# A token mixer on one core: zero products in one run, two blocks' factors made singly, a mask and the last factors later

## The chip, the cores and the metric

One Trainium2 chip, one of its cores. The metric is the device time of one execution in microseconds (us). Five engines work side by side, each through its own queue in order: TensorE (matrix products), VectorE, ScalarE, GpSimd and SyncE (which issues transfers). In the profile they are PE (with PEld for its weight loads), DVE, ACT, POOL and SP.

## The reference, cut to what matters

```python
x = A_x                                   # [1, 2048, 512], bf16
g = sigmoid((x * gate_w).sum(-1))         # a gate for each token
X = rfft2(x) * (w_r + 1j * w_i)
a = irfft2(X)                             # spectral filter over tokens and channels
h = layernorm(x, axis=-1)                 # each token over its 512 channels, eps 1e-5
u = gelu(einsum("bsd,sf->bdf", h, w1) + b1)      # token MLP, 2048 -> 1792
b = (einsum("bdf,fs->bds", u, w2) + b2)          # 1792 -> 2048, transposed back
out = g * a + (1 - g) * b
```

The change touches the layer norm's factors, the order in which normalised blocks are made for the first product of the MLP, and the tables of sines for the transforms.

## The kernel before

The 2048 tokens are 16 blocks of 128 (one token for each of the 128 partitions), 512 channels wide. The schedule is written by hand: an engine runs its instructions in the order in which the program issues them.

**Normalised blocks.** `hn[b]` is block b of the layer norm. VectorE takes the statistics of a block (`bstat`, L246) and joins them to mean and variance (`bn_aggr`, L253). The reciprocal root is a power on GpSimd (L258). Blocks 0 to 5 are normalised on VectorE (`norm_dve`, L271). For blocks 6 to 15 `aggr` and `norm` work on two blocks at a time, and ScalarE makes `hn` (L267) with a scale `rstd` and a bias `nmr` for each token. For the pairs (6, 7) and (14, 15) the constant is added and `nmr` is made on VectorE (L255, L264); for the others both are done on GpSimd, in four small steps: constant (L255), negative mean (L257), power (L258), product (L262).

**First product.** `mm1(b, ft)` multiplies block b of `w1` with `hn[b]` and adds it into column tile `ft` of `u1`. Blocks 0 to 11 go in the order of blocks, eight column tiles each; then each column tile, 0, 2, 4, 6, 1, 3, 5, 7, takes blocks 12 to 15 and goes through GELU on ScalarE (L354). So the first column tile needs blocks 12, 13, 14 and 15 within four products.

**Ahead of it** stand eight products of zeros (`pw`, L240), with one small product among them (`pb`, L239) that turns the first layer's biases into a column. ScalarE copies it to `bcol` (L301).

**Sines.** The transforms need tables `TD` and `TA`. Their angles are whole numbers, cut to a range by a mask on VectorE (`mask`, L195: `md` for TD, `ma` and `mc` for TA), and ScalarE takes the sine (`sines_d`, `sines_a`: L198, L201). These stand between the normalised blocks on ScalarE's queue.

**The gate.** `gprod(q)` (L279) multiplies x with the gate's weights on VectorE, four blocks for each call; ScalarE adds it up later.

Behind the first product TensorE goes through the rest of the first layer (L458), the transforms' products and the second layer (L468, L800) in an order that `fill` and `fill_to` fix by a modelled clock when the program is built.

Of the kernel before, what the change touches and what calls it, by code (L numbers as in the profile page):

```python
# [15 lines left out]
P = 128  # L16
S = 2048
D = 512
NB = 16
# [3 lines left out]
NDVE = 6  # L23
# [20 lines left out]
def kernel(  # L44
# [13 lines left out]
    nc = tc.nc  # L58
# [15 lines left out]
    def pair(name):  # L74
        return psum.tile([P, 2, 512], F32, tag="pair", name=name, bufs=3)

    def bank(name):
        return psum.tile([P, 512], F32, tag="mm", name=name, bufs=2)
# [23 lines left out]
    def gather_w(i):  # L102
        w = (A_w_r, A_w_i)[i]
        for o, src, idx in ((wn[:, i, 8:16].rearrange("p e l -> p (e l)"), w.rearrange("(c e) l -> c (e l)", e=8), 0),
                            (wn[:, i, 16], w, 1)):
            nc.gpsimd.indirect_dma_start(out=o, out_offset=None, in_=src,
                                         in_offset=bass.IndirectOffsetOnAxis(ap=widx[:, idx:idx + 1], axis=0))
# [36 lines left out]
    warm = small.tile([P, P], BF16, name="warm")  # L144
# [14 lines left out]
    def iota(dst, pattern, base, cm=0):  # L159
        nc.gpsimd.iota(dst, pattern=pattern, base=base, channel_multiplier=cm,  # L160
                       allow_small_or_imprecise_dtypes=True)
# [19 lines left out]
    def gather_rows():  # L181
        gp = nc.gpsimd
        iota(widx[:, 0:1], [[0, 1]], 255, -2)
        gp.tensor_scalar(wf[:, 0:1], acol[:, 0:1], 63.5, 1016.0, op0=Alu.is_ge, op1=Alu.mult)
        gp.tensor_scalar(wf[:, 1:2], acol[:, 0:1], 0.5, -1024.0, op0=Alu.is_lt, op1=Alu.mult)
        gp.tensor_scalar(wf[:, 2:3], acol[:, 0:1], -16.0, 2048.0, op0=Alu.mult, op1=Alu.add)
        gp.tensor_add(wf[:, 0:1], wf[:, 0:1], wf[:, 1:2])
        gp.tensor_add(wf[:, 0:1], wf[:, 0:1], wf[:, 2:3])
        gp.tensor_copy(widx[:, 1:2], wf[:, 0:1])
# [4 lines left out]
    def mask(m, n):  # L194
        nc.vector.tensor_single_scalar(m, m, n - 1, op=Alu.bitwise_and)  # L195

    def nsin(dst, m, n):
        nc.scalar.activation(dst, m, ActF.Sin, bias=c_mpi, scale=2.0 * PI_IN / n)  # L198

    def psin(dst, m, n):  # L200
        nc.scalar.activation(dst, m, ActF.Sin, bias=c_pi, scale=-2.0 * PI_IN / n)  # L201
# [5 lines left out]
    def sines_d():  # L207
        nsin(TD[:, :, 1], md[:, 1], 1024)
        nsin(TD[:, :, 2], md[:, 0], 1024)
        psin(TD[:, :, 0], md[:, 0], 1024)  # L210

    def angles_a(v):
        mask(ma[v][:], 2048)
        if v == 0:
            mask(mc[:], 2048)

    def sines_a(v):
        if v == 1:
            nsin(TA[:, :, 1], ma[1][:], 2048)
        else:  # L220
            nsin(TA[:, :, 2], ma[0][:], 2048)
            psin(TA[:, :, 0], ma[0][:], 2048)
            nsin(TA[:, 0, 2, 0:1], mc[:], 2048)
            psin(TA[:, 0, 0, 0:1], mc[:], 2048)
# [9 lines left out]

    pw = bank("pw")
    pb = bank("pb")
    for n in range(8):
        if n == 7:
            nc.tensor.matmul(pb[:, 0:NFT], lhsT=brow[:], rhs=ident[0:NFT, 0:NFT], start=True, stop=True)  # L239
        nc.tensor.matmul(pw[:].rearrange("p (n k) -> p n k", n=4), lhsT=warm[:],  # L240
                         rhs=warm[:, None, :].to_broadcast([P, 4, P]), start=True, stop=True)
    pu = [pair(f"u1_{i}") for i in range(3)]
    u1 = [pu[ft // 2][:, ft % 2] for ft in range(6)] + [bank("u1_6")[:], bank("u1_7")[:]]

    def bstat(b):
        nc.vector.bn_stats(out=stats[:, b, :], in_=xh[b // 8][:, b % 8, :])  # L246

    def on_dve(b):
        return b <= NDVE or b == NB - 2

    def aggr(b0, b1):
        for b in range(b0, b1):
            nc.vector.bn_aggr(out=mv[:, b, :], in_=stats[:, b, :])  # L253
        eng = nc.vector if on_dve(b0) else nc.gpsimd
        eng.tensor_scalar(mv[:, b0:b1, 1], mv[:, b0:b1, 1], 1e-5, 0.0, op0=Alu.add, op1=Alu.add)  # L255
        if not on_dve(b0):
            nc.gpsimd.tensor_scalar(nmr[:, b0:b1], mv[:, b0:b1, 0], -1.0, 0.0, op0=Alu.mult, op1=Alu.add)  # L257
        nc.gpsimd.tensor_tensor(rstd[:, b0:b1], mv[:, b0:b1, 1], c_mhalf.to_broadcast([P, b1 - b0]), op=Alu.pow)  # L258

    def norm(b0, b1):  # L260
        if not on_dve(b0):
            nc.gpsimd.tensor_mul(nmr[:, b0:b1], nmr[:, b0:b1], rstd[:, b0:b1])  # L262
        else:
            nc.vector.scalar_tensor_tensor(nmr[:, b0:b1], mv[:, b0:b1, 0], -1.0, rstd[:, b0:b1],  # L264
                                           op0=Alu.mult, op1=Alu.mult)
        for b in range(b0, b1):
            nc.scalar.activation(hn[:, b, :], xh[b // 8][:, b % 8, :], ActF.Identity,  # L267
                                 bias=nmr[:, b:b + 1], scale=rstd[:, b:b + 1])

    def norm_dve(b):  # L270
        nc.vector.tensor_scalar(hn[:, b, :], xh[0][:, b, :], mv[:, b, 0:1], rstd[:, b:b + 1],  # L271
                                op0=Alu.subtract, op1=Alu.mult)
# [5 lines left out]
    def gprod(q):  # L278
        nc.vector.tensor_mul(prod[q // 2][:, 4 * (q % 2):4 * (q % 2) + 4],  # L279
                             xh[q // 2][:, 4 * (q % 2):4 * (q % 2) + 4],  # L280
                             gwb[:, None, :].to_broadcast([P, 4, D]))
# [30 lines left out]
    for b in range(2, NDVE):  # L312
        bstat(b + 1)
        norm_dve(b)
        if b + 1 < NDVE:
            aggr(b + 1, b + 2)
    for b in range(NDVE, NB, 2):
        if b > NDVE:
            bstat(b)
        if b == NDVE + 2:  # L320
            norm(b - 2, b)
            sines_d()
        bstat(b + 1)
        aggr(b, b + 2)
        if b == NDVE:
            mask(md[:], 1024)
        if b == NB - 2:
            angles_a(1)
        if b > NDVE:
            norm(b, b + 2)  # L330
        if b == NB - 6:
            angles_a(0)
            sines_a(0)
# [3 lines left out]
            mm1(b, ft)  # L337
    for q in range(4):
        gprod(q)
    gather_rows()  # L340
    gather_w(0)
    gather_w(1)
# [30 lines left out]
    for g in range(2):  # L373
        for n, (ps, ms) in enumerate(zip(PLUS[g], MINUS[g])):
            w = 4 // len(PLUS[g])
# [419 lines left out]
    b = NB - 1  # L795
    for h0, h1 in ((0, 256), (256, 384), (384, 512)):
        hs = slice(h0, h1)
        y = bank("yb")
        for ft in range(NFT):
            nc.tensor.matmul(y[:, 0:h1 - h0], lhsT=w2t[b // 2][:, ft, P:2 * P], rhs=gl[:, ft, hs],  # L800
                             start=(ft == 0), stop=(ft == NFT - 1))
# [30 lines left out]
```

## Time and profile before

| | us |
|---|---|
| three timed runs | 128.85, 129.69, 129.98 |
| their median | 129.69 |
| the profiled execution | 128.63 |
| its span (first to last instruction) | 126.7 |
| TensorE busy in it | 122.3 |
| VectorE busy | 111.6 |
| ScalarE busy | 89.7 |
| GpSimd busy | 39.6 |

Times in the profile count from the start of the span. A matrix product's duration holds a modelled end (0.38 us for one of 512 columns, while the next starts 0.216 us behind it), so starts say more than durations. A line of the timeline gives start, duration (from the first start to the last end where several are merged, "x7"), engine, line of the program, operation, out<-in, shapes; in brackets stands the idle time of the engine ahead of it and who ended it.

### The profile page before, as it was taken

To read this page: it belongs to the slowest core of one execution; us is meant where nothing else is said; L and a number is where in the kernel's file an instruction comes from. 1 tells how busy PE (TensorE), PEld (TensorE's weight loads), DVE (VectorE), ACT (ScalarE), POOL (GpSimd) and SP (SyncE) were. 2 spreads that over 40 slices of the span, in tenths; PEclk is the share of its full clock that TensorE was granted. 3 is DMA by queue.
4 is the path that set the end of the run, shared out by engine and by line. 5 is a ranking of instruction groups with operands and counts; after the bars stand their busy time and mean duration, and the time that the engine had idled before them with its cause. 6 is when DMAs were issued, how large, how long until landed. Compare 5 with 4: busy or idle time off the path is not lost.

```text
span 126.7 us, 2074 instructions
## 1 busy us (share of the span) xinstructions
PE 122.3 (97%) x750; PEld 65.2 (51%) x750; DVE 111.6 (88%) x190; ACT 89.7 (71%) x137; POOL 39.6 (31%) x67
## 2 busy tenths in 40 slices
PE   6999999999999999999999999999999999999990
PEld 2244444444444576557764765477644444444480
DVE  4799998999999999999999999999999999993140
ACT  4391299999897699998994799229785599522420
POOL 7133288998887198000040000000000000261200
PEclk9999999999999999999999999999999999999998
DMA  3899999998899999999579206710021101269991
GB/s 95 268 327 379 368 374 352 292 309 262 206 276 121 320 290 293 290 287 291 143 220 294 65 0 190 228 42 0 0 79 50 41 3 41 83 82 201 175 224 29
DMA packets 34635, 24.05 MB, mean 190 GB/s; under 512 B 5536, under 2 KB 32032, under 8 KB 34624
## 3 DMA queue, kind: packets, MB, share of 16 engines
q1 hardware_dynamic: 32516, 21.02, 60.4%
q0 software_dynamic: 1936, 2.76, 13.0%
q8 instruction: 6, 0.10, 0.3%
q10 hardware_dynamic: 172, 0.13, 0.3%
q14 instruction: 5, 0.04, 0.1%
HBM read 19.15 MB, written 3.67 MB: 180 GB/s over the span
## 4 chain that ended last, share of the span: by engine, by line
PE 97%; DVE 0%; issue 0%
PE yb L468 36%; PE u L275 22%; PE u L458 16%; PE ivt L657 5%; PE ivd L673 3%; PE pw L240 3%; PE dp L525 3%; PE yb L800 2%; PE tok L516 2%; PE tok L517 2%; PE ivt L651 0%; PE tok L513 0%; DVE tbv L802 0%; DVE warm L145 0%; PE pb L239 0%
## 5 line engine op out<-in xcount | busy, mean ns | idle before, releaser
L468 PE MATMUL yb<-gl,w2t 128*128 128x512 bf16 x210 | 47.4, 379 | 0.0
L468 PEld LDWEIGHTS <-w2t 128*128 128x128 bf16 x210 | 20.2, 98 | 22.1
L275 PE MATMUL u<-hn,w1a 128*128 128x512 bf16 x128 | 28.5, 385 | 0.0
L458 PE MATMUL u<-hn,w1b 128*128 128x512 bf16 x96 | 23.3, 379 | 0.0
L448 ACT ACTIVATE tbv<-yb,ombb,omg 128x512 bf16<-128x512 f32 x15 | 11.6, 775 | 15.3 <-PE yb L468 15.1
L275 PEld LDWEIGHTS <-w1a 128*128 128x128 bf16 x128 | 12.7, 99 | 15.9 <-issue 1.5
L778 POOL DMA_DIRECT2D out_dram<-ap x3 | 4.0, 1528 | 49.2 <-DVE ap L773 45.3
L458 PEld LDWEIGHTS <-w1b 128*128 128x128 bf16 x96 | 9.0, 98 | 8.0
L286 ACT ACTIVATE junk<-prod 128x512 bf16<-128x512 bf16 x16 | 10.1, 631 | 0.3
L354 ACT ACTIVATE gl<-u,bcol 128x512 bf16<-128x512 f32 x14 | 9.2, 688 | 1.3 <-PE u L458 0.8
L629 ACT CAST R<-ivt 128x1024 bf16<-128x1024 f32 x8 | 7.8, 1038 | 2.3 <-PE ivt L657 2.3
L258 POOL TENSOR_TENSOR rstd<-mv,consts 128x2 f32<-128x2 f32 (+1 forms) x9 | 6.3, 703 | 8.1 <-DVE mv L255 8.0
L629 ACT CAST H<-ivd 128x1024 bf16<-128x1024 f32 x7 | 6.9, 1047 | 0.8 <-PE ivd L673 0.8
L787 DVE TENSOR_TENSOR tbv<-tbv,ap 128x512 bf16<-128x512 bf16 x3 | 1.3, 425 | 5.5 <-ACT tbv L448 5.5
L246 DVE BATCH_NORM_STATS2 stats<-xa 128x6 f32<-128x512 bf16 x8 | 5.5, 686 | 0.5 <-DMA xa<-in_A_x_dram 0.5
L267 ACT ACTIVATE hn<-xb,nmr,rstd 128x512 bf16<-128x512 bf16 x8 | 5.8, 802 | 0.0
L547 DVE TENSOR_TENSOR tatb<-PMA,wn 128x1024 bf16<-128x1024 bf16 x8 | 5.0, 690 | 0.2 <-issue 0.2
L246 DVE BATCH_NORM_STATS2 stats<-xb 128x6 f32<-128x512 bf16 x8 | 5.2, 676 | 0.0
L267 ACT ACTIVATE hn<-xa,nmr,rstd 128x512 bf16<-128x512 bf16 x2 | 1.5, 804 | 5.1 <-DVE nmr L264 5.1
L673 PEld LDWEIGHTS <-R 128*128 128x128 bf16 x64 | 3.8, 98 | 2.5 <-ACT R L629 2.5
L547 DVE TENSOR_TENSOR tatb<-PMB,wn 128x2048 bf16<-128x2048 bf16 x4 | 4.7, 1226 | 0.2
L518 ACT CAST ZA<-tok 128x1024 bf16<-128x1024 f32 x4 | 4.0, 1019 | 1.4 <-PE tok L517 1.3
(198 smaller groups left out, 225.8 us busy)
## 6 DMA issues: line engine op xcount, KB each, us to landing
w2t<-in_B_w_dram SPq DMA_DIRECT2D x8, 896.0 KB, 9.8
w1b<-in_B_w_dram SPq DMA_DIRECT2D x3, 1024.0 KB, 16.3
w1a<-in_B_w_dram SPq DMA_DIRECT2D x2, 1024.0 KB
out_dram<-tbv SPq DMA_DIRECT2D x14, 128.0 KB, 4.0
out_dram<-ap POOLq DMA_DIRECT2D x3, 512.0 KB, 6.8
w1a<-in_B_w_dram SPq DMA_DIRECT2D x4, 256.0 KB, 4.4
w1a<-in_B_w_dram SPq DMA_DIRECT2D x2, 512.0 KB, 8.0
xb<-in_A_x_dram SPq DMA_DIRECT2D x2, 512.0 KB, 7.3
```

What stands on the lines that cost most here:

```text
L246: nc.vector.bn_stats(out=stats[:, b, :], in_=xh[b // 8][:, b % 8, :])
L267: nc.scalar.activation(hn[:, b, :], xh[b // 8][:, b % 8, :], ActF.Identity, bias=nmr[:, b:b + 1], scale=rstd[:, b:b + 1])
L275: nc.tensor.matmul(u1[ft], lhsT=w1a[b // 4][:, b % 4, ft * P:(ft + 1) * P], rhs=hn[:, b, :], start=(b == 0), stop=(b == NB - 1))
L286: nc.scalar.activation(junk[:], prod[b // 8][:, b % 8], ActF.Copy, accum_out=glog[:, b:b + 1])
L354: nc.scalar.activation(gl[:, ft, :], src, ActF.Gelu_apprx_tanh, bias=b1f[:, ft:ft + 1], scale=1.0)
L448: nc.scalar.activation(tbv[0][:, b], y[:], ActF.Identity, bias=gate["ombb2"][:, b:b + 1], scale=gate["omg"][:, b:b + 1])
L458: nc.tensor.matmul(u[:], lhsT=w1b[c][:, b, k * P:(k + 1) * P], rhs=hn[:, b, :], start=(b == 0), stop=(b == NB - 1))
L468: nc.tensor.matmul(y[:], lhsT=w2t[b // 2][:, ft, (b % 2) * P:(b % 2 + 1) * P], rhs=gl[:, ft, :], start=(ft == 0), stop=(ft == NFT - 1))
L547: mul(tt[:, i, :, r:r + n], PM[:, 2 * s:2 * s + 2, r:r + n], w[:, None].to_broadcast([P, 2, n, 256]))
L629: nc.scalar.copy(out, pr[:].rearrange("p h n -> p (h n)"))
L657: nc.tensor.matmul(o[:, 2 * v:2 * v + 2], lhsT=UV[:, 2 * v + c, r, par::2], rhs=TB[:, s, c:c + 2], start=(c == 0), stop=(c == 1))
L673: nc.tensor.matmul(pr[:, c, o * P:(o + 1) * P], lhsT=plane(par, cos), rhs=TI[:, lst, t], start=True, stop=True)
```

## The change

Four edits:

1. The zero products: eight of full width (512 columns) in a row, then the biases' product, then a ninth zero product of half width. Before, the biases' product stood between the seventh and the eighth.
2. Block 6 and block 7 get their factors singly. Block 6 is joined, and its constant added on VectorE, straight behind `norm_dve(5)`; its `nmr` stays on VectorE. Block 7 is joined behind `norm(6)`, and its constant, `nmr` and product go to GpSimd.
3. The mask of `md` moves from behind the aggregates of blocks 6 and 7 to behind those of 8 and 9, and the sines of TD on ScalarE from ahead of `hn[8]` to behind `hn[9]`.
4. `norm(14, 16)`, which makes `nmr` for the last two blocks on VectorE and `hn` on ScalarE, moves out of the loop to behind the first gate product. On ScalarE's queue that is behind the last sines (`sines_a(1)`), which stood behind it before.

```diff
     pw = bank("pw")
     pb = bank("pb")
-    for n in range(8):
-        if n == 7:
+    for n in range(9):
+        w = 4 if n < 8 else 2
+        if n == 8:
             nc.tensor.matmul(pb[:, 0:NFT], lhsT=brow[:], rhs=ident[0:NFT, 0:NFT], start=True, stop=True)
-        nc.tensor.matmul(pw[:].rearrange("p (n k) -> p n k", n=4), lhsT=warm[:],
-                         rhs=warm[:, None, :].to_broadcast([P, 4, P]), start=True, stop=True)
+        nc.tensor.matmul(pw[:, 0:w * P].rearrange("p (n k) -> p n k", n=w), lhsT=warm[:],
+                         rhs=warm[:, None, :].to_broadcast([P, w, P]), start=True, stop=True)
...
     for b in range(2, NDVE):
         bstat(b + 1)
         norm_dve(b)
-        if b + 1 < NDVE:
-            aggr(b + 1, b + 2)
-    for b in range(NDVE, NB, 2):
-        if b > NDVE:
-            bstat(b)
-        if b == NDVE + 2:
-            norm(b - 2, b)
-            sines_d()
+        aggr(b + 1, b + 2)
+    bstat(NDVE + 1)
+    norm(NDVE, NDVE + 1)
+    aggr(NDVE + 1, NDVE + 2)
+    norm(NDVE + 1, NDVE + 2)
+    for b in range(NDVE + 2, NB, 2):
+        bstat(b)
         bstat(b + 1)
         aggr(b, b + 2)
-        if b == NDVE:
+        if b == NDVE + 2:
             mask(md[:], 1024)
         if b == NB - 2:
             angles_a(1)
-        if b > NDVE:
+        if b < NB - 2:
             norm(b, b + 2)
+        if b == NDVE + 2:
+            sines_d()
         if b == NB - 6:
             angles_a(0)
             sines_a(0)
     sines_a(1)
...
     for q in range(4):
         gprod(q)
+        if q == 0:
+            norm(NB - 2, NB)
```

(`NDVE` is 6, `NB` is 16.)

## The prediction

> **What bounds the kernel now.** I read the page first, then the chain of waits, then the timeline of TensorE, ScalarE, VectorE and GpSimd over the first 40 us. The page and its chain:
>
> ```profile
> span 126.7 us, 2074 instructions
> PE 122.3 (97%) x750; PEld 65.2 (51%) x750; DVE 111.6 (88%) x190; ACT 89.7 (71%) x137; POOL 39.6 (31%) x67
> ...
> PE 97%; DVE 0%; issue 0%
> ```
>
> The chain that ended last is TensorE alone. So an edit on another engine counts only where it makes TensorE wait or takes a wait away, and a wait of TensorE, once there, stays to the end. The timeline of TensorE over the first 40 us (start, duration, both in us), and then single pieces of it from narrow windows:
>
> ```profile
> 0.98 3.17 PE L240 MATMUL pw<-warm 128*128 128x512 bf16 x7 [0.98 <-DVE warm L145]
> 4.08 0.19 PE L239 MATMUL pb<-ident,brow 14*128 14x14 bf16 x1
> 4.20 0.61 PE L240 MATMUL pw<-warm 128*128 128x512 bf16 x1
> 4.82 28.50 PE L275 MATMUL u<-hn,w1a 128*128 128x512 bf16 x128
> ```
>
> ```profile
> 4.82 1.01 PE L275 MATMUL u<-hn,w1a 128*128 128x512 bf16 x2
> 6.05 0.63 PE L275 MATMUL u<-hn,w1a 128*128 128x512 bf16 x2
> 15.37 0.59 PE L275 MATMUL u<-hn,w1a 128*128 128x512 bf16 x2
> 15.89 0.38 PE L275 MATMUL u<-hn,w1a 128*128 128x512 bf16 x1
> 26.68 0.38 PE L275 MATMUL u<-hn,w1a 128*128 128x512 bf16 x1
> 26.89 0.38 PE L275 MATMUL u<-hn,w1a 128*128 128x512 bf16 x1
> ```
>
> A duration holds a modelled end, so I go by starts. Seven zero products begin (3.17 - 0.63)/6 = 0.42 us apart; the pair at 4.82 is 1.01 - 0.63 = 0.38 apart; the pair at 6.05 is 0.63 - 0.38 = 0.25 apart; from there all are 0.216 apart. So TensorE runs at half rate until about 6.1 us. The first real product starts at 4.82 because block 0 of hn ends at 4.35 + 0.41 = 4.76 (VectorE, L271). After that there is one hole in the first layer: the second product of the pair at 15.37 starts at 15.58, the next is due at 15.80 and comes at 15.89. It is the first of block 6, and hn of block 6 is what it waits for. The last two lines are the first column's products of blocks 14 and 15: due at 26.68 and 26.89, and not late.
>
> ScalarE, which makes hn from block 6 on:
>
> ```profile
> 15.03 1.52 ACT L267 ACTIVATE hn<-xa,nmr,rstd 128x512 bf16<-128x512 bf16 x2 [5.06 <-DVE nmr L264]
> 16.45 1.10 ACT L198 ACTIVATE TD<-md,consts 128x384 bf16<-128x384 int32 x2
> 17.46 0.60 ACT L201 ACTIVATE TD<-md,consts 128x384 bf16<-128x384 int32 x1
> 17.97 2.92 ACT L267 ACTIVATE hn<-xb,nmr,rstd 128x512 bf16<-128x512 bf16 x4
> 20.79 1.13 ACT L198 ACTIVATE TA<-ma,consts 128x1024 bf16<-128x1024 int32 x1
> 21.83 1.14 ACT L201 ACTIVATE TA<-ma,consts 128x1024 bf16<-128x1024 int32 x1
> ...
> 23.24 2.92 ACT L267 ACTIVATE hn<-xb,nmr,rstd 128x512 bf16<-128x512 bf16 x4
> 26.06 1.14 ACT L198 ACTIVATE TA<-ma,consts 128x1024 bf16<-128x1024 int32 x1
> ```
>
> Block 6 is ready at 15.03 + 0.80 = 15.83, hence the hole at 15.80. From 15.03 ScalarE has no free moment until after 27.2: sines of TD at 16.45, blocks 8 to 11, sines of TA, blocks 12 to 15 (the last ends at 23.24 + 2.92 = 26.16, 0.7 ahead of its use at 26.89), and the last sines at 26.06. One hn starts 0.705 after the one before, one TD sine 0.506, one TA sine 1.04.
>
> **The change, part by part.**
>
> *Zero products.* Eight in a row end at 3.51 + 2 x 0.427 = 4.37. The biases' product came 0.14 after its predecessor could have ended (4.08 against 3.94) and the next product 0.12 behind it: 4.51, 4.63. A half width product at half rate takes 0.213: 4.84. The first real product is then at 4.84 instead of 4.82: +0.02. The copy of the biases on ScalarE (4.31, 0.17 long) moves to about 4.74; the next on its queue is the root for block 1 at 5.62, so nothing waits. What the filled hole (4.63 to 4.82) does to the clock the trace can't say. Bounds: if full rate came at the first real product instead of at 6.1, 1.3 us at half rate would be saved half, 0.65, but block 2 of hn is ready only at 8.27 + 0.41 = 8.68, and block 6 is then reached at 8.74 + 4 x 1.727 = 15.65: -0.24 at most against 15.89. Late: at the end of the span the clock record halves between 125.5 and 125.6, 2.2 behind the last product (123.3); if full rate came that much later, +1.1. I take 0, since the start of the first real product hardly moves.
>
> [...]
>
> *Block 6 alone.* Its mean and variance are joined at 12.67, the constant is added at 12.88 (offsets as at 11.32 and 11.53), GpSimd's power (0.55 for one column) ends at 13.66, VectorE's nmr at 13.86, hn runs 13.90 to 14.70 instead of to 15.83. The hole of 0.09 goes: -0.09 for TensorE up to here.
>
> *Block 7 alone, through GpSimd.* Its aggregate starts 0.08 behind nmr at 13.78 and ends 13.95. GpSimd's four steps are added once more: in the trace, for two columns, they take 1.43:
>
> ```profile
> 17.91 0.23 POOL L255 TENSOR_SCALAR mv<-mv 128x2 f32<-128x2 f32 x1
> 18.21 0.19 POOL L257 TENSOR_SCALAR nmr<-mv 128x2 f32<-128x2 f32 x1
> 18.36 0.70 POOL L258 TENSOR_TENSOR rstd<-mv,consts 128x2 f32<-128x2 f32 x1
> 19.14 0.20 POOL L262 TENSOR_TENSOR nmr<-nmr,rstd 128x2 f32<-128x2 f32 x1
> ```
>
> With 0.55 for the power and 0.09 to get there, nmr of block 7 is ready at 15.36 and hn runs 15.40 to 16.20. TensorE wants it at 17.5: no cost.
>
> *Blocks 8 and 9 ahead of TD's sines.* Two statistics (0.58 and 0.59 apart) from 13.88 on, two aggregates, done at 15.35; the data of block 8 landed before 13.88 (VectorE read it at 14.15 without a wait; the transfer was issued at 6.09 and the median to landing is 7.3). GpSimd begins at 15.44. The mask of md, which now stands behind these aggregates, runs on VectorE from 15.27 to 15.82. In the trace a GpSimd step inside a mask ends with the mask: the product at 17.17 took 0.65 instead of 0.20, mask at 17.11 for 0.66. So the first step ends at 15.87, the last at 17.08, and hn of block 8 starts at 17.12. ScalarE is free from 16.11 and stands idle for 1.0. With no such hold hn 8 starts at 16.91; with a second step held (+0.45) and a slow power (0.94 instead of 0.70, the row at 13.86), 17.8; with no wait for GpSimd at all, 16.11. I take 17.12. Blocks 10 and 11: their aggregates come when they came before (mask 0.46 later, everything else 0.4 earlier), and nmr is ready at 19.0, ahead of ScalarE.
>
> *The end of ScalarE's row.* From hn 8 on ScalarE is busy without a hole, but two things now stand between hn 8 and hn 15 that stood outside: TD's three sines (3 x 0.506 = 1.52, were ahead of hn 8) and the last TA sine (1.04, was behind hn 15: the call that makes blocks 14 and 15 is now behind the one for the last sines). hn 8 begins 17.97 - 17.12 = 0.85 earlier. So hn 15 ends at 26.16 + 1.52 + 1.04 - 0.85 = 27.87 instead of 26.16, hn 14 at 27.16. Their factors are no limit: the first gate product (1.22) stands ahead of nmr on VectorE, and even if the power waits for it, nmr is ready near 23.
>
> **What is late next.** TensorE's first column of block 14 waits until 27.22, that of block 15 until 27.87 + 0.06 = 27.93, where 26.89 stood: **+1.04**. It is one wait: the other seven columns read the same four blocks. Bounds by hn 8 at 16.11 and 17.8: +0.03 and +1.7. Behind the wait, ScalarE's table load and GELUs start at 29.2 instead of 28.5; the fourth frees the bank for the second part of the first layer at 31.6, which TensorE wants at 34.2, so nothing more is late. VectorE fills the 0.58 in which it waited for GpSimd (before 22.04) and is half a us earlier into the transforms, which TensorE doesn't wait for. SP's transposes of TD and TA were issued at 31.30, behind the weights' transfers, and TA is done at 27.2 in both orders: unmoved. GpSimd's gathers follow its last power by up to 0.8 later; they have until the weights' products, some 20 us behind.
>
> **Sum.** +0.02 - 0.09 are swallowed, for the later wait is set by ScalarE's clock time: +1.04. Against the profiled execution, 128.63 us with a span of 126.7 (1.93 lies around it): 129.67. That execution is 1.06 faster than the median of the runs shown, 129.69 (128.85 to 129.98). If the median's extra lies in TensorE's first 26 us (a later full rate), the new wait swallows it: 129.7. If it lies elsewhere, 130.7. Nothing here shows which; a late clock would need nearly its whole bound of 1.1, so I lean four to one to the second: **130.5**, +0.6%.
>
> **Rivals.**
> - *A: hn 15 isn't late, and the change gains.* If GpSimd delivers block 8's factors by 16.11, hn 15 ends at 26.86 and TensorE starts at 26.92 at the latest; with full rate early and the hole at 15.80 gone, up to -0.24: 129.45. It decides at an arrival of the factors 1.0 earlier than I find. Against it: four steps that take 1.43 start when two statistics are done, which leaves no room. Chance 0.14.
> - *B: the wait costs the clock.* TensorE stands for some 0.5 twice within 1.2 us; if that makes the rate fall, and half rate lasts as long as at the start (0.98 to 6.1, 5.1), 2.6 are lost on top: 129.69 + 1.04 + 2.6 = 133.3. For it: 2.2 without products halve the clock at the end. Against it: the holes near 3.9 and 4.7 didn't prevent full rate, and the new ones are a quarter of 2.2 each. Chance 0.12. [...]
> - *C: GpSimd's chain is held more than once* (hn 8 at 17.8): +1.7, 131.4. For it: three of the six powers and products near masks were slow. Chance 0.12.
>
> **How the numbers follow.** Forecast 0.62, A 0.14, B 0.12, C 0.12. About 1% (1.3 us) is what a measurement of this kernel tells from no change. The forecast, with half the spread shown (0.55) around 130.5, lies mostly under 130.99: 0.47 same, 0.15 slower. B and C are slower. A is 0.09 same, 0.05 faster, which needs the spread as well. Sum: faster 0.05, same 0.56, slower 0.39. The range runs from A's 129.45, less a little, to C's 131.4, plus a little: 129.3 to 131.7; B is left out.
>
> **What would show it.** Right: hn of block 6 done near 14.7 and no hole at 15.8; ScalarE idle ahead of hn 8 until about 17.1; order TA sine, hn 14, hn 15 with the end near 27.9; the first column's products of blocks 14 and 15 near 27.2 and 27.9, 0.216 spacing else. Wrong: hn 8 before 16.5; no wait at block 15; spacings of 0.43 after 30 us; or a wait behind 34 us that the page of before doesn't have.

## The result and the profile after

The changed kernel is slower: 129.71 us against 128.81 us (medians of 22 runs each, 129.16 to 130.44 and 128.26 to 129.98), ratio 1.0067, 95% interval 1.0049 to 1.0085; of 128.81 us that is 0.86, with an interval of 0.63 to 1.09. The profiled execution took 129.98 us with a span of 128.1, so the two profiled ones differ by 1.35. Ratios and their intervals, here and below, leave out executions more than 1.5% slower than the fastest of the same kernel.

The page of the changed kernel (busy times and, below, the engines' shares of the chain that ended last):

```profile
span 128.1 us, 2080 instructions
PE 122.4 (96%) x751; PEld 64.9 (51%) x751; DVE 111.6 (87%) x190; ACT 89.9 (70%) x137; POOL 40.3 (31%) x71
...
PE 75%; ACT 8%; DMA 6%; SPq 4%; DVE 1%; POOL 1%; issue 1%
```

TensorE's busy time is what it was (122.3), yet it is 75% of the chain where it was 97%. The rest, read backwards, is ScalarE, GpSimd, VectorE, a transfer of x and SyncE, which issued it (SPq): the chain now leaves TensorE once, ahead of the first column's product of block 15. The timeline of TensorE shows it (in brackets: idle time and who ended it):

```profile
0.98 3.31 PE L241 MATMUL pw<-warm 128*128 128x512 bf16 x8 [0.98 <-DVE warm L145]
4.22 0.18 PE L240 MATMUL pb<-ident,brow 14*128 14x14 bf16 x1
4.33 0.28 PE L241 MATMUL pw<-warm 128*128 128x256 bf16 x1
4.72 7.54 PE L276 MATMUL u<-hn,w1a 128*128 128x512 bf16 x32
12.60 14.54 PE L276 MATMUL u<-hn,w1a 128*128 128x512 bf16 x66 [0.34 <-DMA w1a<-in_B_w_dram]
27.48 0.38 PE L276 MATMUL u<-hn,w1a 128*128 128x512 bf16 x1 [0.34 <-ACT hn L268]
28.19 2.10 PE L276 MATMUL u<-hn,w1a 128*128 128x512 bf16 x9 [0.33 <-ACT hn L268]
```

The first column's products of blocks 14 and 15 start at 27.48 and 28.19; they stood at 26.68 and 26.89. By starts (the last product before them begins at 26.76), TensorE loses 0.50 ahead of each. In this execution it lost some time before that as well, among it 0.51 at 12.60, where a transfer of weights was late; it was then in no hurry, since block 15 came at 28.19 whatever it had done. ScalarE's timeline, and two lines each of VectorE and GpSimd:

```profile
15.29 0.81 ACT L268 ACTIVATE hn<-xa,nmr,rstd 128x512 bf16<-128x512 bf16 x1 [0.67 <-POOL nmr L263]
17.38 1.52 ACT L268 ACTIVATE hn<-xb,nmr,rstd 128x512 bf16<-128x512 bf16 x2 [1.28 <-POOL nmr L263]
18.80 1.10 ACT L198 ACTIVATE TD<-md,consts 128x384 bf16<-128x384 int32 x2
...
25.59 1.13 ACT L198 ACTIVATE TA<-ma,consts 128x1024 bf16<-128x1024 int32 x1
26.63 1.50 ACT L268 ACTIVATE hn<-xb,nmr,rstd 128x512 bf16<-128x512 bf16 x2
```

```profile
14.08 1.29 DVE L247 BATCH_NORM_STATS2 stats<-xb 128x6 f32<-128x512 bf16 x2 [0.23 <-DMA xb<-in_A_x_dram]
...
15.50 0.53 DVE L195 TENSOR_SCALAR md<-md 128x768 int32<-128x768 int32 x1
```

```profile
13.95 0.24 POOL L256 TENSOR_SCALAR mv<-mv 128x1 f32<-128x1 f32 x1 [0.37 <-DVE mv L254]
...
15.67 0.45 POOL L256 TENSOR_SCALAR mv<-mv 128x2 f32<-128x2 f32 x1 [0.42 <-DVE mv L254]
```

ScalarE, which makes the normalised blocks `hn` from block 6 on, stands idle for 1.28 ahead of block 8, starts it at 17.38, and from there has no hole until block 15 is done at 26.63 + 1.50 = 28.13. TD's sines (18.80) and the last TA sine (25.59) now lie inside that stretch. The start at 17.38 comes from VectorE, which waited 0.23 for the transfer of block 8, and from GpSimd, whose first step took 0.45 while the mask ran on VectorE (for block 7, without a mask, it took 0.24).

### The profile page after: what moved, and what is told of

The parts are those of the page before. It is cut to its first block, busy times and chain, and to the rows that moved or that the text cites. A ratio compares the mean times of both kernels' runs of the same rounds, so it can differ in the third digit from the quotient of the medians.

```text
span 128.1 us, 2080 instructions
## 1 busy us (share of the span) xinstructions
PE 122.4 (96%) x751; PEld 64.9 (51%) x751; DVE 111.6 (87%) x190; ACT 89.9 (70%) x137; POOL 40.3 (31%) x71
## 4 chain that ended last, share of the span: by engine, by line
PE 75%; ACT 8%; DMA 6%; SPq 4%; DVE 1%; POOL 1%; issue 1%
PE yb L472 35%; PE u L462 16%; DMA xb<-in_A_x_dram 6%; PE u L276 5%; PE ivt L661 5%; ACT hn L268 4%; PE ivd L677 3%; PE dp L529 3%; PE yb L804 2%; PE tok L520 2%; PE tok L521 2%; SPq L90 2%; SPq L93 2%; ACT TA L198 2%; ACT TA L201 1%
## 5 line engine op out<-in xcount | busy, mean ns | idle before, releaser
L259 POOL TENSOR_TENSOR rstd<-mv,consts 128x1 f32<-128x1 f32 (+1 forms) x10 | 6.5, 654 | 7.3 <-DVE mv L256 7.1
L601 POOL TENSOR_SCALAR omg<-g__762 128x16 f32<-128x16 f32 x1 | 0.6, 590 | 14.9 <-ACT g__762 L599 14.9
L677 PE MATMUL ivd<-TI,R 128*128 128x128 bf16 x64 | 4.9, 220 | 0.0
```

Source lines behind the costliest of these rows:

```text
L677: nc.tensor.matmul(pr[:, c, o * P:(o + 1) * P], lhsT=plane(par, cos), rhs=TI[:, lst, t], start=True, stop=True)
```

## The experiments

Theory S: ScalarE's row of work from block 8 to block 15 sets the wait, with TD's sines (1.52) and the last sines (1.04) put into it. Rival Z: the new order of the zero products, or the clock, costs the time. Rival G: the steps that GpSimd now takes for block 7 alone cost it. Each ratio is to the kernel before, run on the same chip.

**Each late edit undone.** First the last blocks, ahead of the last sines again:

```diff
         gprod(q)
-        if q == 0:
-            norm(NB - 2, NB)
...
-        if b < NB - 2:
-            norm(b, b + 2)
+        norm(b, b + 2)
```

> The changed kernel with its fourth edit undone: the last two blocks go ahead of the last sines again; the other three edits stay. Theory S (ScalarE's row sets the wait at block 15: TD's sines behind hn 8 add 1.52, the last sines ahead of hn 14 add 1.04): hn of block 15 ends 1.04 earlier than in the changed kernel (28.13 - 1.04 = 27.09), TensorE would get there at about 26.9 to 27.2, so the wait all but goes: 0 to 0.3 us over before, ratio 1.000 to 1.002. Rival Z (the zero products' order or the clock costs the 0.9): stays at 1.007. Rival G (block 7's own steps on GpSimd delay all that follows, whatever the order at the end): stays near 1.007, with hn of block 15 late all the same.

Measured 1.0017 (0.9991 to 1.0044), 128.89 us. Most of the loss is gone; what is left agrees with 0 to 0.3 us. In its profile block 15 still holds TensorE for 0.45, as block 8 started at 17.80 in that execution: there block 6 was already 0.77 later than in the changed kernel's (14.57 instead of 13.80).

Then mask and sines of TD ahead of block 8, the last blocks left late:

```diff
     norm(NDVE + 1, NDVE + 2)
+    mask(md[:], 1024)
+    sines_d()
     for b in range(NDVE + 2, NB, 2):
...
-        if b == NDVE + 2:
-            mask(md[:], 1024)
...
-        if b == NDVE + 2:
-            sines_d()
```

> The changed kernel with its third edit undone: mask of md and TD's sines stand ahead of hn 8 again, in ScalarE's idle time; the last two blocks stay behind the last sines. Theory S: hn 8 starts behind the sines at 17.5 (17.38 in the changed kernel), so hn 15 ends 1.52 - 0.13 = 1.4 earlier, at 26.74, just ahead of its use: ratio 0.998 to 1.001. Rivals Z and G: 1.007.

Measured 1.0020 (1.0000 to 1.0039), 128.71 us. Its ScalarE timeline:

```profile
16.61 1.11 ACT L198 ACTIVATE TD<-md,consts 128x384 bf16<-128x384 int32 x2
...
18.15 3.05 ACT L268 ACTIVATE hn<-xb,nmr,rstd 128x512 bf16<-128x512 bf16 x4
...
26.00 1.50 ACT L268 ACTIVATE hn<-xb,nmr,rstd 128x512 bf16<-128x512 bf16 x2
```

TD's sines fill the idle time; block 8 starts only 0.77 later than in the changed kernel (18.15), and block 15 ends 0.63 earlier (27.50). Two things stand behind the 0.77: block 6 was 0.39 later in this execution (14.19), and the mask, now ahead of block 8's statistics, runs on VectorE during GpSimd's first step for block 7, which took 0.46 instead of 0.24. So block 7 starts at 15.89 instead of 15.29, with TD's sines behind it. I had left that second hold out: the 1.4 that I expected is 0.63 here, and the time shows a rest of 0.2%.

Both undone, only the first two edits left:

> Edits one and two alone: zero products in one run and blocks 6 and 7 singly; sines, mask and last blocks as before. Theory S: no wait at block 15 (hn 15 ends near 25.7), hole of 0.09 at block 6 gone: 0 to 0.24 us faster than before, ratio 0.998 to 1.000. Rival Z and rival G: 1.007.

Measured 1.0013 (0.9994 to 1.0032), 128.63 us. The loss is gone, against Z and G, which both have their edit in it. But nothing is gained either. In its profile TensorE no longer waits for a block of ScalarE; by starts it waits 0.25 for block 1 (until 6.83) and 0.21 for block 2 (until 8.77), which VectorE makes. From there it goes on at 0.216 and reaches block 6 at 15.67, 0.22 earlier than in the profile before, and so it stays to the end of TensorE's work; the timed runs show nothing of it.

**One part at a time, on the kernel before.** The first edit alone:

> The kernel before with the first edit alone (eight zero products in a row, the biases' product, a ninth of half width). Theory S: nothing behind the first real product changes; 0.02 us, ratio 0.999 to 1.001. Rival Z (the filled hole changes when full rate comes): a change of 0.2 us or more one way or the other, ratio under 0.998 or over 1.002.

0.9993 (0.9960 to 1.0025), 128.81 us: no effect that can be told, against Z; an effect of 0.2 us is inside the interval and stays open. Two of its thirteen runs, 131.21 and 132.77, are outside the ratio; the second is told of below. The fourth edit alone, and the third alone:

> The kernel before with the fourth edit alone: the last two blocks behind the last sines and behind the first gate product. Theory S: hn 15 ends at 26.16 + 1.04 = 27.20, TensorE wants it at 26.83: about +0.37 us, ratio 1.003 (1.001 to 1.004). Rivals Z and G: the edits that they blame are not in it, so 1.000.

1.0023 (0.9997 to 1.0050), 129.00 us; one of twelve runs, outside the ratio, took 132.80.

> The kernel before with the third edit alone: mask of md and TD's sines behind hn 9, blocks 6 and 7 as a pair. Theory S: GpSimd's factors of block 8 are ready near 17.3, hn 8 starts then (17.97 before), TD's 1.52 come behind it, hn 15 ends at 26.16 + 1.52 - 0.62 = 27.06; the slack of 0.67 that it has before is used up and 0.23 us more: ratio 1.002 (1.000 to 1.004). Rival G (block 7 alone is what costs): 1.000, with hn 15 no later than before.

1.0022 (0.9993 to 1.0052), 129.00 us. Its profile has the start of block 8 that was expected near 17.3, and the wait at block 15, which is 0.48 by starts where 0.23 was expected:

```profile
17.34 1.52 ACT L267 ACTIVATE hn<-xb,nmr,rstd 128x512 bf16<-128x512 bf16 x2 [1.06 <-POOL nmr L262]
```

```profile
27.11 5.14 PE L275 MATMUL u<-hn,w1a 128*128 128x512 bf16 x22 [0.32 <-ACT hn L267]
```

Both intervals reach 1, so neither is shown by itself; together they are:

```diff
-        if b > NDVE:
+        if NDVE < b < NB - 2:
             norm(b, b + 2)
+        if b == NDVE + 2:
+            sines_d()
...
         gprod(q)
+        if q == 0:
+            norm(NB - 2, NB)
```

> The kernel before with the third and the fourth edit, without the first two: both operations on ScalarE (TD's sines 1.52, last sines 1.04) come between hn 8 and hn 15, blocks 6 and 7 stay a pair. Theory S: hn 15 has a slack of 0.67 in the kernel before, which is paid once; so the two together cost more than their sum alone (1.0023 and 1.0022): hn 8 near 17.35 as with the third edit alone, hn 15 at 27.06 + 1.04 = 28.1, ratio 1.007 to 1.010, like the changed kernel or a little over it. If the costs just add: 1.0045. Rival G (block 7's own steps on GpSimd are part of the cost): under the changed kernel's 1.0067, near 1.0045.

Measured 1.0087 (1.0044 to 1.0130), 129.77 us. The middle is about twice the sum of the two alone, as a slack that is used up once demands; the interval's lower end touches the sum, so this is in favour and not proof. In its profile the first column's product of block 15 starts at 28.20, against 28.19 in the changed kernel. The loss is there without block 7's steps: G falls.

**More work in the stretch, and ahead of it.** One more ScalarE operation of 1.13, first ahead of block 14, then ahead of block 8:

```diff
         if q == 0:
+            nc.scalar.activation(ma[1][:], krow[:], ActF.Identity, bias=consts[:, 4:5], scale=acol[:, 0:1])
             norm(NB - 2, NB)
```

> The changed kernel with one more ScalarE operation ahead of hn 14: the angles of the last sines written once more (1.13 from start to start; nothing reads them). Theory S: all of it lies on the path: hn 15 ends 1.13 later, 1.13 us over the changed kernel, ratio to before 1.0155 (1.013 to 1.018). Rival: if another engine set the wait, ScalarE has room there and it costs less than 0.3: 1.007 to 1.009.

Measured 1.0151 (1.0122 to 1.0179), with one run of the lower clock told of below in it and two such runs left out. The four runs in which the clock held took 130.65 to 130.98, about 1.0 over the changed kernel's 129.71, and in the profile block 15's product starts at 29.24, 1.05 later. All but some 0.1 of the operation lies on the path.

```diff
+        if b == NDVE + 2:
+            nc.scalar.activation(ma[1][:], krow[:], ActF.Identity, bias=consts[:, 4:5], scale=acol[:, 0:1])
         if b < NB - 2:
             norm(b, b + 2)
```

> The changed kernel with the same extra ScalarE operation (1.13) ahead of hn 8, where ScalarE waits 1.28 for GpSimd. Theory S: it fits into the idle time, 0 us over the changed kernel, ratio to before 1.0067 (1.005 to 1.009), hn 8 again near 17.4. Rival: if only the sum of ScalarE's work counted and not where it stands, 1.13 more, 1.0155.

Measured 1.0092 (1.0064 to 1.0121) in four runs, 129.95 us. That is not the 1.0155 of the rival; the changed kernel's 1.0067 is at the low end of the interval. In the profile the operation fills the idle time, and block 8 starts no later than in the changed kernel's:

```profile
16.12 1.23 ACT L330 ACTIVATE ma<-krow,consts,acol 128x1024 int32<-128x1024 f32 x1
17.25 1.50 ACT L268 ACTIVATE hn<-xb,nmr,rstd 128x512 bf16<-128x512 bf16 x2
```

By the medians the same operation costs 1.0 in one place and 0.24 in the other, which by the profile may be nothing: where work stands in ScalarE's row is what counts.

**Does the wait cost the clock?** The clock share of a run is the mean rate granted to TensorE, as a part of the full one. With the operation ahead of block 14, three of seven runs had a share of 0.987 and took 132.31 to 133.09, by medians 1.9 more than the other four; of the 75 runs of the kernel before that were timed beside these experiments none was under 0.994. Two kernels follow that up. In the first, nine products with zero weights stand where TensorE waits; in the second, ScalarE's operation stands there twice.

```diff
         for b in range(12, NB):
+            if ft == 0 and b == 14:
+                for _ in range(9):
+                    nc.tensor.matmul(u1[0], lhsT=warm[:], rhs=hn[:, 0, :], start=False, stop=False)
             mm1(b, ft)
```

> The kernel with one more operation ahead of hn 14, and nine products with zero weights (1.94 us) on TensorE between the first column's blocks 13 and 14, added to the same sum, where TensorE waited 2.1. With the wait open the clock share was 0.987 in 3 of 7 runs (half rate for 3.4 us) and the time 1.7 more in these. Theory W (the wait drops the clock): with the wait filled the clock share stays at 0.994 or more in all runs and the time is that of the others, 130.7 to 131.1. Rival N (the clock drops at times without a cause in the kernel): 0.987 comes about as often, 3 of 7.

Ratio 1.0127 (1.0069 to 1.0184); six runs, 130.62 to 131.67 (median 130.76), clock share 0.996 or more in all. No run has the drop, which alone, six runs against seven, could still be chance.

```diff
         if q == 0:
+            nc.scalar.activation(ma[1][:], krow[:], ActF.Identity, bias=consts[:, 4:5], scale=acol[:, 0:1])
+            nc.scalar.activation(ma[1][:], krow[:], ActF.Identity, bias=consts[:, 4:5], scale=acol[:, 0:1])
             norm(NB - 2, NB)
```

> The changed kernel with two more ScalarE operations (1.13 each) ahead of hn 14. Theory S: 2.26 us over the changed kernel, ratio to before 1.024 where the clock holds. Theory W: TensorE waits 3.2 before block 14, and the clock share is 0.987 in more than half of the runs, 1.7 us more in these. Rival N: no more often than with one operation, and rarely.

Ratio 1.0329 (1.0249 to 1.0409). Five of six runs had a share of 0.987 or less (133.83 to 135.97). Two of these had 0.974 and 0.975, twice the drop, and were the slowest (135.53 and 135.97). One run held the clock and took 132.64, 2.9 over the changed kernel where 2.26 were expected; it is a single run, and the profile has block 15's product 2.36 later. Five of six with the long wait against none of six with the wait filled, on one chip: theory W stands. The wait in the kernel with one operation, and one in the kernel with the first edit alone, whose profiled run took 132.77:

```profile
28.53 0.38 PE L276 MATMUL u<-hn,w1a 128*128 128x512 bf16 x1 [1.90 <-ACT hn L268]
```

```profile
54.90 4.47 PE L459 MATMUL u<-hn,w1b 128*128 128x512 bf16 x13 [2.45 <-DMA w1b<-in_B_w_dram]
```

Stretches of TensorE around the drop, first in the kernel with one operation, then in that with two, then in that with the first edit alone (columns: stretch in us, its length, busy time of TensorE with the instructions, granted clock, share and rate of the transfers):

```profile
26.19:29.60 3.41, 1.19 (x6) 1.00 1.15 305
29.61:33.02 3.41, 3.41 (x10) 0.50 0.82 251
```

```profile
26.49:29.90 3.41, 0.30 (x3) 1.00 1.04 278
29.91:33.31 3.40, 3.25 (x8) 0.50 0.78 225
```

```profile
51.13:54.53 3.40, 1.32 (x15) 1.00 1.19 292
54.55:57.94 3.39, 3.04 (x8) 0.50 1.20 292
```

The stretches at half rate (granted clock 0.50) are 3.39 to 3.41 long here, and in the 3.40 or 3.41 behind each the clock was 1.00 again. In the 3.40 or 3.41 ahead of them TensorE was busy for 0.30 to 1.32. In the last, TensorE waited 2.45 for a transfer of weights, at 52 to 55 us, far from what the first edit touches. None of the 22 runs of the changed kernel, with two waits of 0.5, has such a share, and none of the twelve with the third and fourth edits, whose profile has 0.72 and 0.49 by starts. The run of 132.80 with the fourth edit alone had a share of 0.987 too; it left no trace, so its cause stays open.

None of the eleven versions was measurably faster than the kernel before.

## Why the prediction was right

The direction and the mechanism held, and the size of the main term: +1.04 us forecast, 0.86 measured, with 1.04 inside its interval. The base that it was added to was off. That the +0.6% on record comes so near the +0.67% measured is partly luck: it is a mean of 130.7 (+1.04 on the base of 129.69) and 129.7 (no change), weighted four to one, and the sum by itself says +0.8%.

- **The end of ScalarE's row**, the term that carries the sum: +1.52 + 1.04 - 0.85, with hn 15 at 27.87 and TensorE at 27.93. The profile has 28.13 and 28.19. That is 1.30 behind the 26.89 of the profile before, where the timed runs differ by 0.86; why the two profiles lie further apart than the runs is open. Undoing either half takes most of the loss away, and adding work there costs nearly its full length.
- **The start of block 8**, forecast 17.12: it was 17.38 in the changed kernel's profile, and 17.16 to 17.80 in others with the same order. The step that failed in that profile is "the data of block 8 landed before 13.88": the transfer, issued at 6.01, landed near 14.05, VectorE waited 0.23, and the whole row moved by that. In the kernels with one and with two operations ahead of block 14 VectorE didn't wait there, and block 8 starts at 17.16 and 17.19, behind 0.93 and 0.94 of idle time on ScalarE instead of 1.28. The hold by the mask came as worked out (0.45 instead of 0.24).
- **Zero products**: forecast +0.02, hidden; measured none within 0.4%. The first real product came at 4.72. Full rate came at about 3.9, 2.9 us behind the first zero product, where the profile before has about 6.1, 5.1 behind: the zero products up to 3.51 start 0.42 apart, the one at 3.91 took 0.38 where the first took 0.61, and the real ones are 0.216 apart from 4.72 on. What sets the moment of full rate no run shows.
- **Swallowed gains**: -0.09 at block 6 and an early clock were to vanish behind the later wait, and did. In the changed kernel's profile TensorE also lost some 0.5 to a late transfer of weights without cost. The kernel with the first two edits alone, where no such wait stands, was put at 0 to 0.24 us faster; its profile has 0.22 at block 6, and its runs show no gain.
- **The base** is the step that was mis-sized. I leaned four to one to adding +1.04 to the median of three runs, 129.69. Two of these three were the slowest of the 22 runs, whose median is 128.81, close to the profiled 128.63. The sum against the profiled execution, 129.67, meets the measured 129.71; the 130.5 on record is 0.8 too high.
- **Rival B** was right as a mechanism and wrong on this kernel: its price was put at 2.6, with half rate for 5.1. One drop lasted 3.41 (29.61 to 33.02 in the kernel with one operation ahead of block 14), and runs with one took 1.9 more by medians in that kernel, 1.2 to 1.4 more than a single run with two. The shortest single wait seen ahead of a drop is 1.90, as the timeline gives it; the kernel with the operation ahead of block 8 has one of 0.72 and kept its clock in four runs, and nothing between the two was tried. **Rival C** didn't come: one GpSimd step ahead of block 8 was held, not two. **Rival A** needed factors by 16.11; they came at about 17.34.

## What to carry to other kernels

When an engine off the critical path feeds the one on it, look for the last item that it must deliver and count what stands between its last idle moment and that item. Work moved from ahead of the idle moment to behind it, or from behind the item to ahead of it, is paid, less the slack of that item, and the slack is paid once however many edits use it. Here 1.05 of an operation of 1.13 ahead of block 14 was paid at block 15's product (29.24 instead of 28.19), and nothing there of the same operation ahead of block 8 (28.05). Filling such an idle time cost little or nothing here; emptying it did cost, though every moved operation was the same as before.

## What the runs showed of the hardware that was not expected

In three profiles TensorE's rate was half (granted clock 0.50) for 3.39 to 3.41 us at a single wait of 1.90, 2.45 or 3.10, as the timelines give them: in the kernel with one operation ahead of block 14, in the one with the first edit alone and in the one with two operations. It fell 1.1 behind the end of the first of these waits, 0.4 before the end of the second and 0.1 behind that of the third. In the 3.40 or 3.41 us ahead of the drop TensorE was busy for 1.19, 1.32 and 0.30; in the changed kernel's profile full rate came at the end of a stretch of 3.40 (0.46 to 3.86) in which it was busy for 2.88. The kernel with one operation dropped its clock in three of seven runs; what sets these three apart no run shows. With nine products of zero weights in the gap, none of six runs dropped it.
